# Attention, then a SiLU MLP, on one core: one burst of 64x64 tiles per pair and eight shared PSUM banks

## The chip, the cores and the metric

The kernel runs on one core of one Trainium2 chip. The metric is the device time of one execution in microseconds (us). The kernel before takes 217.31 us, the median of three runs (216.69 to 217.38). TensorE is PE below, VectorE is DVE, ScalarE is ACT, GpSimd is POOL, and SP is the queue that issues most loads.

## The reference

A causal linear attention with decay feeds an MLP with a SiLU. There are 4 batches, 8 heads, 768 positions and a head dimension of 64.

```python
for b in range(nb):                      # blocks of 64 positions
    intra = einsum('bhic,bhjc->bhij', qb, kb) * Dmask
    intra = einsum('bhij,bhjd->bhid', intra, vb)
    inter = einsum('bhid,bhde->bhie', qb * lam_pow, kv_state)
    out[:, :, sl] = intra + inter
    kv_state = lam_block * kv_state + einsum('bhsd,bhse->bhde', kb * rev_pow, vb)
x = out.transpose(0, 2, 1, 3).reshape(3072, 512)
h = x @ w_in                             # 512 -> 2048
return (h * sigmoid(h)) @ w_out          # 2048 -> 512
```

Inputs and output are float32; the kernel's matmuls take bfloat16.

## The kernel before

**Tiling.** Attention works on blocks of 128 positions, two of them (chunks) to a "pair" of 256. There are 12 pairs, three to a batch, and 24 units of 128 tokens for the MLP. For a pair, `prepare` casts k and q into `kq` and scales v into `vd`. It turns k and q into `kqT`: pairs 0 to 3 by PE transposes through a PSUM bank, later pairs by a DMA transpose. `attention` then issues these tiles on PE:

- states (`states`, line 499): 32 matmuls of 64x64 with 64 columns, k against v. The third pair of a batch is final and needs 16.
- scores (`score`, line 561): twice 16 matmuls of 64x64 with 128 columns, k against q. DVE multiplies each half by a triangle into `st` (`mask`, line 566, through the helper at line 300).
- inter (`inter`, line 588): full 128x128 matmuls with 128 columns, q against the carried state in `xe`, which holds two heads on the diagonal of a 128x128 block with zeros beside them.
- outputs (`outputs`, line 598): twice 16 matmuls of 64x64 with 128 columns, v against the masked scores, into the same accumulators as inter. DVE scales them into `xt` (`evac`, line 612).

DVE makes the state chain out of states: `y` is the sum with the carried state (line 527), `xe` the scaled state for inter, `xf` the scaled state for the next chunk.

**The MLP.** `product1` (line 634) forms 2048 hidden columns for a group of 256 or 512 tokens, one PSUM bank at a time, and ACT applies SiLU into `g` (line 650). `product2` (line 670) multiplies a unit by `w_out` in 16 matmuls of 512 columns into one bank. DVE or ACT copies it to `osb`, and ACT's queue stores it.

**PSUM.** Of eight banks, four are a pool `bank`. Two are `st2` for scores, and two are `xd` for inter, outputs and, in other columns, states.

**Order.** `Planner.order` lists the work by an event simulation. Each task has a cost per engine, a key, dependences, and buffers from small pools. An engine that comes free takes the ready task with the lowest key that has its buffers. The resulting order is fixed, and each engine runs its instructions in that order. In the key, attention of pair n stands at about 2n - 5.5, product 1 of a unit u at about u, and product 2 at about u + 4. The planner charges a switch between full matmuls and 64x64 tiles. Loads go through SP's queue in the order of `sequence`, the halves of `w_out` through POOL's queue. `occupy` (line 701) puts matmuls on ones into planned gaps of the first 19 us, but only where the next task's bank has not been written yet.

The keys of outputs and scores are close, so the planner often puts outputs of one unit beside scores of a later one:

```python
de = add((s - 0.7, 0, 2, g) if n else (s - 0.6, 1, g), ... states ...)
sc = add((s + g - 0.7, 0, 3) if i else (s - 0.55, 0), ... score ...)
im = add((s + g + 0.3, 0, 0), ... inter ...)
om = add((s + g + 0.3, 0, 1), ... outputs ...)
```

Of the kernel before, what the change touches and what calls it, by code (L numbers as in the profile page):

```python
# [14 lines left out]
class Task:  # L15
    __slots__ = ("key", "on", "deps", "bufs", "fn", "left", "ready", "end", "users", "nbytes", "kind", "prior", "next", "late")
# [9 lines left out]
class Buf:  # L26

    __slots__ = ("pool", "slot", "left", "tile", "with_")

    def __init__(self, pool, with_=None):  # L30
        self.pool, self.slot, self.left, self.tile, self.with_ = pool, None, 0, None, with_
# [6 lines left out]
class Planner:  # L38
# [6 lines left out]
    SWITCH = 0.095  # L45
    FIRST, LAST, AHEAD = {"SP": 1.15, "ACT": 1.15, "POOL": 3.0}, 1.0, 0.75

    def __init__(self, pools):
        self.pools = {n: list(range(c)) for n, c in pools.items()}
        self.tasks = []  # L50

    def add(self, key, on, fn, deps=(), bufs=(), nbytes=0, kind=None, prior=(), late=0.0):
        key = key if isinstance(key, tuple) else (key,)
        t = Task(key, on, fn, deps, list(bufs) + [b.with_ for b in bufs if b.with_], nbytes, kind, prior, late)
        for b in t.bufs:
            b.left += 1
        self.tasks.append(t)
        return t

    def order(self):  # L60
# [11 lines left out]
        started = set()  # L72
        queues = {e: [] for e in ("SP", "POOL", "ACT")}
        tiled = False
# [50 lines left out]
        while len(out) < len(self.tasks):  # L125
# [6 lines left out]
            while release and release[0][0] <= now:  # L132
                _, _, b = heapq.heappop(release)
                self.pools[b.pool].append(b.slot)
            for e in free:
# [7 lines left out]
                kept, took = [], None  # L143
                while ready[e]:
# [15 lines left out]
                    break  # L160
                for k in kept:
                    heapq.heappush(ready[e], k)
# [4 lines left out]
                for b in t.bufs:  # L167
                    if b.slot is None:
                        b.slot = self.pools[b.pool].pop(0)
                free[e] = now + t.on[e]  # L170
# [24 lines left out]
def kernel(  # L195
# [22 lines left out]
    TIED = 4  # L218
    AWAY, XAWAY, OWN = ((1, 0),), (), (0, 1)
    WKEY, WCAST, WON = -2.0, {"POOL": 1.0, "ACT": 0.6, "DVE": 0.43}, [("POOL", "ACT", "DVE")] * 2 + [("POOL", "DVE"), ("POOL", "ACT")]  # L220
    FIRST_ONES, ONES_UNTIL = 11, 19.0
# [6 lines left out]
    POOLS = dict(bank=4, st2=1, xd=1, raw=11, rawh=6, kq=4, kqT=3, vd=3, st=2, xe=4, y=2, xf=3,  # L228
                 xt2=4, xt4=2, g=40, osb=3, osh=4, one=3, two=2)
    plan = Planner(POOLS)  # L230
    add = plan.add

    def tile_of(b, shape, dt, name):
        if b.tile is None:
            pool = ps if b.pool in ("bank", "st2", "xd") else sb
            b.tile = pool.tile(shape, dt, tag=f"{b.pool}{b.slot}", name=name)
        return b.tile
# [31 lines left out]
    nc.vector.memset(xe_all, 0.0)  # L269
    pose = const.tile([128, 2], F32, name="pose")  # L270
# [56 lines left out]
    def load_pair(key, n, which):  # L327
# [8 lines left out]
        for g, ms in enumerate(parts_of(n)):  # L336
            for i in which:
                bufs[i, g] = Buf("rawh" if n in FINE else "raw")
                ts[i, g] = add((key, g, i), {"SP": 0.55}, lambda e, i=i, g=g, ms=ms: plain(e, i, g, ms), bufs=[bufs[i, g]],
                               nbytes=0.131 * len(ms), kind=WIDE, late=0.3 if n < EARLY else LATE)  # L340
# [3 lines left out]
    def load_w(key, what, j):  # L344
# [7 lines left out]
        for h in range(KI // 2):  # L352
# [5 lines left out]
            t = add((key, 0, h), {"SP": 0.55}, half, bufs=[b], nbytes=0.5243, kind=PLAIN, late=0.1)  # L358
            for ko in (2 * h, 2 * h + 1):
                wload[what, j, ko] = add((WKEY + j, ko), {e: WCAST[e] for e in WON[j]},  # L360
                                         lambda e, b=b, ko=ko: copy(e, w_in_bf[:, ko, cs], b.tile[:, ko % 2]), deps=[t], bufs=[b])
# [47 lines left out]
    def xe_of(b):  # L409
        return xe_all[:, b.slot]  # L410

    def duo_tile(i):
        return tile_of(duo_of[i][0], [128, 2, 512], F32, "xd")
# [3 lines left out]
    def prepare(n):  # L417
# [21 lines left out]
        for g, ms in enumerate(parts):  # L439
            w = len(ms) / 4  # L440
            ck.append([add((s - 1.0, g, i), {"DVE": 0.06 + 0.8 * w, "ACT": 0.17 + 0.9 * w}, lambda e, i=i, g=g: cast(e, i, g),
                           deps=[loads[i, g]], bufs=[bufs[i, g], kq]) for i in range(2)])
            after("k", ck[g])
            cv.append(add((s - 0.8, g), {"POOL": 0.1 + 2.6 * w} if (n, g) in AWAY else {"DVE": 0.12 + 1.15 * w}, lambda e, g=g: scale_v(e, g), deps=[loads[2, g]],
                          bufs=[bufs[2, g], vd]))
            after("v", [cv[g]])

        if n < EARLY:
            def turn(e, bank, i, r, m):
                t = tile_of(bank, [128, 2, NP, U], BF16, "tr")  # L450
                nc.tensor.transpose(t[:, r, m, :], kq_of()[:, i, r, 2 * m:2 * m + 2, :], ident)  # L451

            for g, ms in enumerate(parts):
                w = len(ms) / 4
                turned.append([])
                for i in range(2):
                    bank = Buf("bank")
                    ts = [add((s - 0.7, g, i, r, m), {"PE": 0.056}, lambda e, i=i, r=r, m=m, bank=bank: turn(e, bank, i, r, m),
                              deps=[ck[g][i]], bufs=[bank, kq]) for r in range(2) for m in ms]
                    turned[g].append(add((s - 1.0, 2, g), {"DVE": 0.15 + 1.05 * w, "ACT": 0.17 + 0.85 * w},  # L460
                                         lambda e, i=i, bank=bank, ms=ms: copy(e, t_of()[:, i, :, ms[0]:ms[-1] + 1],
                                                                               bank.tile[:, :, ms[0]:ms[-1] + 1]),
                                         deps=ts, bufs=[bank, kqT]))
# [9 lines left out]

    def attention(n):
# [3 lines left out]
        tied = []  # L478
        if TIED < n + 1 < NU // 2:
            tied = ready_of[n + 1][5][0] + ready_of[n + 1][4]  # L480
# [3 lines left out]
        final = blk == NB - 1  # L484
        own = [Buf("bank"), Buf("bank")] if n in OWN else None
        buf, box = ([], set()) if own else duo(2 * n - 1)
        bufs_d = own or [buf]

        def d_tile(c):
            return tile_of(own[c], [128, 512], F32, "d0")[:, :256] if own else duo_tile(2 * n - 1)[:, c, 256:512]  # L490
# [3 lines left out]
        def states(e, ms):  # L494
            for m in ms:
# [8 lines left out]
        xes = [Buf("xe") for _ in range(1 if final else 2)]  # L504
# [5 lines left out]
        for g, ms in enumerate(parts):  # L510
            w = len(ms) / 4
            de = add((s - 0.7, 0, 2, g) if n else (s - 0.6, 1, g), {"PE": 0.28 * w}, lambda e, ms=ms: states(e, ms), bufs=bufs_d + [kq, vd], kind="tiled",
                     deps=[ck[g][0], cv[g]] + mask_of.get(2 * n - 1, []) + outs.get(2 * n - 1, []))
            sl = slice(ms[0], ms[-1] + 1)
            old = (prev[2][0], last_f) if prev else None
            for c in range(len(xes)):
# [6 lines left out]
                if old:  # L523
                    src = ys[c]

                    def new_y(e, src=src, old=old, d_of=d_of, sl=sl):
# [3 lines left out]
                    sd = [add((s + late - 0.9, 1, g), {"DVE": 0.15 + 0.27 * w}, new_y, deps=[de] + old[1], bufs=[dbuf, src, old[0]])]  # L530
                    so = lambda src=src, sl=sl: src.tile[:, sl]
                b = xes[c]
                made[c] += [add((s + late - 0.9, 2, g), {"POOL": 0.1 + 0.6 * w} if (n, c) in XAWAY else {"DVE": 0.13 + 0.28 * w},
                                lambda e, b=b, so=so, h=h, d=d, sl=sl: mult(e, xe_of(b)[d, sl, 64 * h:64 * h + 64], so()[d],
                                                                             rate[d, sl]),
                                deps=sd, bufs=[src, b]) for h, d in enumerate(halves)]
                if not final:
# [3 lines left out]
                            deps=sd, bufs=[src, f])  # L541
# [4 lines left out]
        if not final:  # L546
            carry[n] = xe[2] + ((xfs[1], fs),)


        half = []  # L550
        for g in range(2):
# [3 lines left out]
            def score(e, g=g, st_ps=st_ps):  # L555
                t = tile_of(st_ps, [128, 2, 2, 2, U], F32, "st_ps")
# [8 lines left out]
            def mask(e, st_ps=st_ps, st=st):  # L565
                mult(e, tile_of(st, [128, 4, 4 * 64], BF16, "st"), st_ps.tile.rearrange("p h m r i -> p (h m) (r i)"),
# [3 lines left out]
                     + (made[0] + made[1] if g and n >= TIED else []), bufs=[st_ps, kqT],  # L570
                     kind="tiled")
            mask_of[i] = [add((s + g - 0.9, 0), {"DVE": 1.25}, mask, deps=[sc], bufs=[st_ps, st])]
# [4 lines left out]
        for g in range(2):  # L577
# [6 lines left out]
            def inter(e, i=i, g=g, used=used, box=box_x):  # L584
                t = duo_tile(i)
                for m in range(2):
# [5 lines left out]
            def outputs(e, i=i, g=g, st=st, box=box_x):  # L592
                t = duo_tile(i)
                for m in range(2):
# [152 lines left out]
```

## Time and profile before

| what | value |
|---|---|
| median of three runs | 217.31 us (216.69 to 217.38) |
| the profiled execution | 217.49 us |
| its span, first to last instruction | 215.6 us |
| mean granted PE clock | 0.984 |
| busy: PE, DVE, ACT, POOL | 205.8, 105.6, 104.3, 19.9 us |
| product 1 on PE (line 634) | 130.0 us in 566 records |
| product 2 on PE (line 670) | 122.0 us in 386 records |
| mask on DVE, 128x1024 | 24 of 1218 ns |
| xt on DVE, 128x512 | 24 of 689 ns |

Matmuls are pipelined, so durations of one group overlap, and their sum is more than the time that PE gives them. Distances between starts say what a matmul costs: in a row, a 512-column matmul comes every 0.216 us and a 256-column one every 0.109 us. A few per cent of the matmul records are missing, and such a hole looks like a wait of about that length.

### The profile page before, as it was taken

Reading aid. Unit: us, or ns where it says so; the run is one execution under the profiler, and the core shown is the slowest. Engines: PE = TensorE matmul, PEld = TensorE weight load, DVE = VectorE, ACT = ScalarE, POOL = GpSimd, SP = SyncE. Lnnn points to the kernel's source line nnn. Section 1 sums busy time; section 2 is a strip of 40 time slices with the busy share of each in tenths; the row PEclk is TensorE's granted clock in tenths of the full one; section 3 lists DMA queues with packets and bytes.
Section 4 is the critical chain, followed back from the end, with each engine's and each line's share of the span. In section 5 each row is a group of like instructions: output and inputs, shape, how many; then the busy total and the mean of one; then the engine's idle time right before and its main releaser. Section 6 shows DMA issues by size and latency. Waiting matters only on the chain.

```text
span 215.6 us, 5080 instructions
## 1 busy us (share of the span) xinstructions
PE 205.8 (95%) x2243; PEld 124.8 (58%) x2267; DVE 105.6 (49%) x161; ACT 104.3 (48%) x151; POOL 19.9 (9%) x34
## 2 busy tenths in 40 slices
PE   7789999999999999999999999999999999999993
PEld 2567788877656566668755545455444444444452
DVE  3888969961728366978958683154111100111000
ACT  4758697955523351547664342442444444444121
POOL 4041326100300000104001030000000000000000
PEclk9967999999999999999999999999999999999999
DMA  4999999999999896999990610110111011110212
GB/s 128 334 381 381 321 348 279 206 216 256 235 349 240 231 351 152 304 269 282 228 287 3 149 52 0 49 52 0 49 52 49 9 40 49 50 53 0 97 49 97
DMA packets 62182, 35.98 MB, mean 167 GB/s; under 512 B 18000, under 2 KB 57168, under 8 KB 62160
## 3 DMA queue, kind: packets, MB, share of 16 engines
q1 hardware_dynamic: 56304, 27.27, 46.9%
q10 hardware_dynamic: 3744, 6.30, 7.8%
q0 software_dynamic: 2112, 2.10, 6.0%
q8 instruction: 17, 0.28, 0.5%
q14 instruction: 5, 0.04, 0.0%
HBM read 27.27 MB, written 6.29 MB: 156 GB/s over the span
## 4 chain that ended last, share of the span: by engine, by line
PE 92%; DVE 4%; issue 2%; ACT 1%; DVEq 0%
PE h_ps L634 39%; PE o_ps L670 38%; PE xd L598 4%; PE idle L705 3%; PE st_ps L561 2%; PE xd L588 2%; PE tr L451 2%; DVE st L300 1%; PE xd L499 1%; DVE xe_all L300 1%; DVE xt L300 1%; ACT g L650 0%; DVE y L527 0%; DVE vd L300 0%; PE d L499 0%
## 5 line engine op out<-in xcount | busy, mean ns | idle before, releaser
L634 PE MATMUL h_ps<-xt,w_in_bf 128*128 128x256 bf16 (+1 forms) x566 | 130.0, 307 | 1.0 <-ACT g L650 0.2
L670 PE MATMUL o_ps<-w_out_bf,g 128*128 128x512 bf16 (+1 forms) x386 | 122.0, 370 | 1.3 <-issue 1.0
L650 ACT ACTIVATE g<-h_ps 128x512 bf16<-128x512 f32 x96 | 70.7, 747 | 83.4 <-PE h_ps L634 81.7
L634 PEld LDWEIGHTS <-w_in_bf 128*128 128x128 bf16 x576 | 55.1, 98 | 29.7 <-issue 0.5
L670 PEld LDWEIGHTS <-g 128*128 128x128 bf16 x400 | 39.1, 98 | 40.6
L300 DVE TENSOR_TENSOR st<-st_ps,tri 128x1024 bf16<-128x1024 f32 x24 | 29.2, 1218 | 14.1 <-PE st_ps L561 14.0
L300 DVE TENSOR_TENSOR xt<-xd,lam_xe 128x512 bf16<-128x512 f32 x24 | 16.5, 689 | 26.5 <-PE xd L598 13.7
L295 DVE COPY osb<-o_ps 128x512 f32<-128x512 f32 x11 | 7.6, 690 | 40.8 <-PE o_ps L670 40.8
L300 POOL TENSOR_TENSOR xf<-y,lam_be 128x256 f32<-128x256 f32 (+1 forms) x12 | 9.9, 822 | 100.2 <-DVE y L527 100.2
L300 DVE TENSOR_TENSOR xe_all<-y,lam_be 64x256 bf16<-64x256 f32 (+1 forms) x34 | 18.4, 540 | 0.6
L293 ACT ACTIVATE osb<-o_ps 128x512 f32<-128x512 f32 (+1 forms) x14 | 7.9, 561 | 15.1 <-PE o_ps L670 14.8
L300 DVE TENSOR_TENSOR vd<-raw,lam_v 128x1024 bf16<-128x1024 f32 (+1 forms) x12 | 14.0, 1163 | 0.5 <-DMA raw<-in_v_dram 0.5
L293 ACT ACTIVATE kq<-raw 128x1024 bf16<-128x1024 f32 (+1 forms) x12 | 12.1, 1010 | 1.9 <-ACT osb L293 0.8
L293 ACT ACTIVATE kqT<-tr 128x1024 bf16<-128x1024 bf16 (+1 forms) x10 | 8.5, 851 | 4.9 <-PE tr L451 4.7
L705 PE MATMUL idle<-ones 128*128 128x128 bf16 (+1 forms) x59 | 9.2, 319 | 1.7 <-DVE ones L247 1.5
L598 PE MATMUL xd<-st,vd 64*64 64x128 bf16 x384 | 10.5, 229 | 0.0
L561 PE MATMUL st_ps<-kqT 64*64 64x128 bf16 x384 | 10.1, 222 | 0.2
L295 DVE CAST kq<-raw 128x1024 bf16<-128x1024 f32 (+1 forms) x14 | 8.8, 629 | 2.9 <-DMA raw<-in_k_dram 2.5
L588 PE MATMUL xd<-kqT,xe_all 128*128 128x128 bf16 x80 | 8.6, 221 | 0.5 <-DVE xe_all L300 0.4
L588 PEld LDWEIGHTS <-xe_all 128*128 128x128 bf16 x80 | 6.5, 99 | 4.1 <-DVE xe_all L300 0.6
L527 DVE TENSOR_TENSOR y<-xd,xf 128x256 f32<-128x256 f32 x13 | 5.4, 418 | 6.2 <-PE xd L499 5.6
L561 PEld LDWEIGHTS <-kqT 64*64 64x64 bf16 x384 | 6.9, 109 | 2.0 <-issue 1.6
(40 smaller groups left out, 63.0 us busy)
## 6 DMA issues: line engine op xcount, KB each, us to landing
out_dram<-osb ACTq DMA_DIRECT2D x23, 256.0 KB, 2.4
raw<-in_k_dram SPq DMA_DIRECT2D x11, 512.0 KB, 6.1
raw<-in_q_dram SPq DMA_DIRECT2D x11, 512.0 KB, 6.8
raw<-in_v_dram SPq DMA_DIRECT2D x11, 512.0 KB, 6.1
raw_w<-in_moe_w_in_dram SPq DMA_DIRECT2D x8, 512.0 KB, 7.4
w_out_bf<-in_moe_w_out_dram POOLq DMA_DIRECT2D x4, 512.0 KB, 13.1
raw<-in_k_dram SPq DMA_DIRECT2D x2, 256.0 KB, 4.8
raw<-in_q_dram SPq DMA_DIRECT2D x2, 256.0 KB, 5.0
```

The lines of the kernel that those rows point to most:

```text
L293: nc.scalar.activation(o, i, AF.Copy)
L295: nc.vector.tensor_copy(o, i)
L300: (nc.vector if e == "DVE" else nc.gpsimd).tensor_tensor(o, a, b, op=AL.mult)
L451: nc.tensor.transpose(t[:, r, m, :], kq_of()[:, i, r, 2 * m:2 * m + 2, :], ident)
L527: nc.vector.tensor_tensor(tile_of(src, [128, NP, 64], F32, "y")[:, sl], d_of(), old[0].tile[:, sl], op=AL.add)
L561: nc.tensor.matmul(t[c, h, m, r, :], lhsT=t_of()[d, 0, r, 2 * g + m, c], rhs=t_of()[d, 1, :, 2 * g + m, c], start=(m == 0 and r == 0), sto ...
L588: nc.tensor.matmul(t[:, c, U * m:U * m + U], lhsT=xe_of(x[0])[:, 2 * g + m, :], rhs=t_of()[:, 1, :, 2 * g + m, halves[c]], start=first_in( ...
L598: nc.tensor.matmul(t[d, c, U * m:U * m + U], lhsT=vd.tile[p, 2 * (2 * g + m) + h, r, :], rhs=st.tile[p, 2 * h + m, U * r:U * r + U], start ...
L634: nc.tensor.matmul(t[:, j, :], lhsT=w_in_bf[:, ko, 128 * m:128 * m + 128], rhs=xt[gi].tile[:, ko, :], start=(ko == 0), stop=(ko == KI - 1))
L650: nc.scalar.activation(t, bank.tile.rearrange("p j (c r a) -> p (j c) r a", c=n // U, r=2), AF.Silu)
L670: nc.tensor.matmul(t, lhsT=g.tile[:, j, 128 * gp:128 * gp + 128], rhs=w_out_bf[:, ko, cs], start=(ko == 0), stop=(ko == KO - 1))
L705: nc.tensor.matmul((t[:, 0] if two else t)[:, 0:w], lhsT=ones[:, 0:128], rhs=ones[:, 0:w], start=True, stop=True)
```

## The change

1. From pair 3 on, one `burst` per pair replaces the separate tasks. It holds inter and outputs of the pair before, then states and scores of its own pair. Each half of the array's rows has a list of its own: rows 0 to 63 states of chunk 0, outputs of chunk 0, scores of the even heads, and rows 64 to 127 outputs of chunk 1, states of chunk 1, scores of the odd heads. The two lists are merged by their running length. The burst is cut into three tasks that follow each other: up to the last output, up to the last score of the first two head pairs, and the rest.
2. Outputs of pair 3 stand in a burst alone (`SOLO`). A last burst has only outputs of pair 11.
3. States of both chunks share one bank, and scores take four. `fence` puts a PE `nop` that waits for the last matmul of chunk 0 ahead of the first state of chunk 1. Masks become four of 128x512 per pair, one per bank.
4. PSUM is one tile of eight banks. When `st2` and `xd` have had their last use, the planner adds their four banks to `bank`. A burst that lacks banks holds back tasks that would take one, except a product 2 when no bank is half filled. Product 1 leaves the last free bank if anything else can go.
5. In pairs 0 and 1 the first state uses are compact: `xs` is 64 columns wide and has no zeros, one DVE instruction makes it instead of two, and inter is 64x64 tiles in two passes with a fence ahead of outputs.
6. v of pair 1 is scaled on DVE and no more on POOL. A few keys are shifted and two casts are given an engine. The SiLU table is loaded by a task of its own. `occupy` uses any vacant bank, and its count per gap is larger. `g` has 36 buffers for 40, and `st` 4 for 2.

```diff
+    SHIFT = {('xe', 0, 0, 1): 4.5, ('load w', 3, 1): -1.5, ('scale', 3, 0): -1, ('xe', 3, 0, 0): 1.5}
+    HOME = {('cast', 3, 0, 1): 'ACT', ('cast w', 1, 3): 'POOL'}
...
+                if not last[b.pool] and b.pool in self.becomes:
+                    to, slots = self.becomes[b.pool]
+                    self.pools[to] += slots
...
                     if any(len(self.pools[p]) < n for p, n in need.items()):
+
+                        held |= t.kind == "burst" and all(len(self.pools[p]) >= n for p, n in need.items() if p != "bank")
+                        kept.append((key, i, t))
+                        continue
+                    if held and "bank" in need and (opened or t.kind != "p2"):
+                        kept.append((key, i, t))
+                        continue
+                    if self.scarce and t.kind == "p1" and "bank" in need and len(self.pools["bank"]) < 2:
+                        spare = spare or (key, i, t)
                         kept.append((key, i, t))
                         continue
...
-    TIED = 4
-    AWAY, XAWAY, OWN = ((1, 0),), (), (0, 1)
-    WKEY, WCAST, WON = -2.0, {"POOL": 1.0, "ACT": 0.6, "DVE": 0.43}, ...
-    FIRST_ONES, ONES_UNTIL = 11, 19.0
+    TIED, SOLO = 3, (3,)
+    AWAY, XAWAY, OWN = (), (), (0, 1)
+    SMALL = (0, 1)
+    WKEY, WCAST, WON = -2.0, {"POOL": 0.75, "ACT": 0.62, "DVE": 0.45}, ...
+    FIRST_ONES, ONES_UNTIL = 10, 19.0
...
+    plan = Planner(POOLS, {"st2": ("bank", [4, 5]), "xd": ("bank", [6, 7])})
+    banks = ps.tile([128, 8, 512], F32, name="banks")
...
+    def fence(done):
+
+        tc.add_manual_dep(nc.tensor.nop(nofuse=True).ins, done[-1].ins.name, mybir.DependencyInfo(
+            mybir.DependencyClass.Sync, mybir.DependencyReason.DATA), reason="rows of one bank")
...
+    def burst(n, alone=False):
...
+            def state(k, r, c):
+                if c and not k and not r:
+                    fence(at_zero)
...
+        if new:
+            queue(0, "d", 64, state, 0)
+        if o:
+            queue(0, "o", 128, output, 0)
+            queue(1, "o", 128, output, 1)
+        elif new:
+            queue(1, "s", 128, score, 1)
+        if new:
+            if not final:
+                queue(1, "d", 64, state, 1)
+            queue(0, "s", 128, score, 0)
+            if o:
+                queue(1, "s", 128, score, 1)
...
+                ts.append(add((2 * n - 8.5 - alone, j), {"PE": order[cut - 1][3] - spent}, go, deps=[t for t in ts[-1:] if t] or deps, bufs=bufs, kind="burst",
+                              tag=("burst", n - alone / 2, j)))
...
-        xes = [Buf("xe") for _ in range(1 if final else 2)]
+        xes = [Buf("xs" if n + c in SMALL else "xe") for c in range(1 if final else 2)]
...
+                if n in SMALL:
+
+                    for y in (1, 0):
+                        for m in range(2):
+                            for c, x in used:
+                                d = halves[y ^ c]
+                                mm = nc.tensor.matmul(t[d, c, U * m:U * m + U], lhsT=xe_of(x[0])[d, 2 * g + m, :],
+                                                      rhs=t_of()[d, 1, :, 2 * g + m, halves[c]],
+                                                      start=first_in(box, c, y ^ c), stop=True, skip_group_check=True)
...
+    table = add((-3.0, 0), {"ACT": 1.28}, lambda e: nc.scalar.preload_act_table_set("silu_and_others"),
+                deps=[lam_x] + ready_of[1][3][0], tag="table")
...
+            elif start < ONES_UNTIL and start - at > 0.15:
+                b = vacant(at, start)
+                if b:
+                    occupy(b, int((start - at) / 0.056 * 0.75), 128)
```

More of the change, by code (lines that the diff above doesn't have):

```diff
@@ L15 @@
 class Task:
-    __slots__ = ("key", "on", "deps", "bufs", "fn", "left", "ready", "end", "users", "nbytes", "kind", "prior", "next", "late")
+    __slots__ = ("key", "on", "deps", "bufs", "fn", "left", "ready", "end", "users", "nbytes", "kind", "prior", "next", "late", "tag")
     def __init__(self, key, on, fn, deps, bufs, nbytes=0, kind=None, prior=(), late=0.0):
@@ L72, in order @@
         started = set()
+        last = {}
+        for t in self.tasks:
+            for b in t.bufs:
+                last.setdefault(b.pool, set()).add(id(b))
+        opened = set()
         queues = {e: [] for e in ("SP", "POOL", "ACT")}
-        tiled = False
+        tiled = self.scarce = False
         clock = [0.0]
@@ L142, in order @@
                     continue
-                kept, took = [], None
+                kept, took, held, spare = [], None, False, None
                 while ready[e]:
@@ L160, in order @@
                     break
+                if took is None and spare and not held:
+                    kept.remove(spare)
+                    took = spare[2]
                 for k in kept:
@@ L593, in outputs @@
                 t = duo_tile(i)
+                follow(i)
                 for m in range(2):
@@ L631, in mm @@
             def mm(e, j, ko, bank=bank, mg=mg):
-                t = tile_of(bank, [128, per, n], F32, "h_ps")
+                t = psum_of(bank).rearrange("p (j n) -> p j n", j=per)
                 m = mg * per + j
@@ L668, in mm @@
                 g, j, _ = gs[gi, ko]
-                t = tile_of(bank, [128, w], F32, "o_ps")
-                nc.tensor.matmul(t, lhsT=g.tile[:, j, 128 * gp:128 * gp + 128], rhs=w_out_bf[:, ko, cs],
+                nc.tensor.matmul(psum_of(bank)[:, :w], lhsT=g.tile[:, j, 128 * gp:128 * gp + 128], rhs=w_out_bf[:, ko, cs],
                                  start=(ko == 0), stop=(ko == KO - 1))
```

261 lines of the change are left out of this document (200 added, 61 removed).

## The prediction

> **What bounds the kernel now.** I read the shares and the chain first, then busy time by stretch, then the order of time on TensorE (PE) in the middle and on VectorE (DVE) early. Page, part 4, the chain that ended last:
>
> ```profile
> PE 92%; DVE 4%; issue 2%; ACT 1%; DVEq 0%
> ```
>
> The stretches (time in the stretch, busy us and instruction count of each engine, granted PE clock, DMA share, GB/s):
>
> ```profile
> 9.00:12.40 3.40, 1.86 (x53) 1.31 (x53) 2.89 (x8) 2.94 (x6) 0.40 (x1) 0.98 1.13 342
> 12.40:19.10 6.70, 6.28 (x87) 5.01 (x87) 5.71 (x11) 3.88 (x6) 1.90 (x1) 0.50 1.07 386
> 19.10:25.30 6.20, 5.73 (x122) 4.32 (x119) 6.05 (x9) 4.89 (x7) 2.09 (x3) 1.00 1.08 360
> 25.30:45.00 19.70, 19.70 (x332) 16.77 (x329) 16.93 (x28) 15.75 (x24) 5.94 (x9) 1.00 1.11 272
> 45.00:155.00 110.00, 108.13 (x1304) 66.03 (x1321) 64.04 (x91) 50.74 (x70) 7.34 (x8) 1.00 0.71 180
> 155.00:212.30 57.30, 56.88 (x293) 27.41 (x295) 5.53 (x8) 20.98 (x31) 0.00 (x0) 1.00 0.12 47
> ```
>
> From 25.3 us on PE is full, so a microsecond counts there only if PE issues less or switches less. From 12.4 to 25.3 DVE is busy 11.76 of 12.9 us, and PE's clock is 0.50 until 19.1.
>
> What attention costs PE in the middle stands in the order of time: start, duration, instruction.
>
> ```profile
> 64.23 0.27 PE L634 MATMUL h_ps<-xt,w_in_bf 128*128 128x256 bf16 x1
> 64.43 0.42 PE L561 MATMUL st_ps<-kqT 64*64 64x128 bf16 x16
> 64.78 0.39 PE L670 MATMUL o_ps<-w_out_bf,g 128*128 128x512 bf16 x1
> ...
> 83.63 0.38 PE L670 MATMUL o_ps<-w_out_bf,g 128*128 128x512 bf16 x1
> 83.84 0.39 PE L588 MATMUL xd<-kqT,xe_all 128*128 128x128 bf16 x4
> 84.16 0.42 PE L598 MATMUL xd<-st,vd 64*64 64x128 bf16 x16
> 84.41 0.42 PE L499 MATMUL xd<-vd,kq 64*64 64x64 bf16 x32
> 84.66 0.40 PE L561 MATMUL st_ps<-kqT 64*64 64x128 bf16 x16
> 84.99 0.61 PE L634 MATMUL h_ps<-xt,w_in_bf 128*128 128x256 bf16 x2
> ```
>
> I call such a run of attention tiles between MLP matmuls a visit. From start to start, 16 outputs or 32 states take 0.25 us, four inter matmuls 0.22. The second visit takes 84.99-83.84 = 1.15 and holds 0.22+3x0.25 = 0.97, so 0.18 goes to entering and leaving the 64x64 form. The lone score visit delays the MLP by 64.78-64.23-0.11 = 0.44 us for one group of 0.25: 0.19. If the groups themselves shrink to the 0.227 that four-deep matmuls would need (16x0.0568/4), the price of a visit is 0.24. I take 0.21.
>
> **Part by part.** The sum is made against the profiled execution: 217.49 us, span 215.6 and 1.9 around it. The median of the three runs shown is 217.31, 0.18 less.
>
> *Bursts, pairs 3 to 11.* Before, these pairs' states, scores, inter and outputs make 23 visits between 37.6 and 155 us. After, there are 11: states and scores of pair 3, outputs of pair 3 alone, states and scores of pair 4, seven full bursts, the last outputs. No matmul goes away. 12 visits x 0.21 = -2.5 us, all on the path since PE is full; bounds -2.2 (0.18) and -2.9 (0.24). In a burst the two row halves run their own lists at once, 64-wide states beside 128-wide outputs. At 76.97 us before, row-0 states and scores of the other row half already overlap in the records, so I keep the array time equal. Masks become four of 128x512 instead of two of 128x1024. The same shape costs 0.69 in the xt groups against 1.22, so DVE gets 4x0.69-2x1.22 = +0.3 us per pair. This is hidden: DVE is busy 64 of 110 us there, and would cost 2.8 us in all were it not.
>
> *The fence in a burst.* States of chunk 1 write the bank of chunk 0's, so a PE nop waits for the last chunk-0 state. It sits in PE's own order, so every output, score and MLP matmul behind it waits too. That state starts about 0.20 us into the tiled part and lasts 0.193 (the states' group), so it ends at 0.39. DVE starts 0.04 to 0.09 after a PE end in this trace, giving 0.43 to 0.48; the outputs ahead of the nop keep row 1 busy until 8x0.0568 = 0.454. No wait of PE on itself is in the trace. Bounds: 0, and one whole states duration, 0.19. A gain is excluded, as nothing is removed. Six bursts have chunk-1 states (final pairs don't): 0 to +1.2 us; I take 0.05 each, +0.3, because the row arithmetic almost covers it.
>
> *Seven banks at once.* A full burst takes two output banks, one for states and four for scores, of eight. While it lacks banks the planner starts no product-1 bank, and a product-2 bank only if none is open. What must drain is a SiLU (0.747 us), an osb copy (0.59 or 0.69), or masks of the forerunner, long done some 12 us later. An open product-2 bank is 16x0.216 = 3.5 us of PE work, longer than any drain. Behind a burst DVE frees banks at 0.69 us each, outputs first; product 1 fills one in 8x0.109 = 0.87. So bounds are 0 and one SiLU plus hop, 0.85, for each of seven full bursts: 6 us. The nearest row is PE waiting for ACT g once, 0.2 us in all. I take +0.4.
>
> *First pairs.* With compact states, pair 0's eight 64x128 products into xe_all become four of full height, and pair 1's first chunk one 128x256 (0.42) instead of two:
>
> ```profile
> 13.69 1.90 POOL L300 TENSOR_TENSOR vd<-raw,lam_v 128x1024 bf16<-128x1024 f32 x1 [1.40 <-DMA raw<-in_v_dram]
> ...
> 14.17 1.56 DVE L300 TENSOR_TENSOR xe_all<-y,lam_be 64x128 bf16<-64x128 f32 x1
> ...
> 21.01 1.58 DVE L300 TENSOR_TENSOR xe_all<-y,lam_be 64x256 bf16<-64x256 f32 x2
> ```
>
> Four halves at 0.286 (the rows from d) saved: -1.1. At 21.0, 1.58 becomes 0.42 to 0.8: -0.9. Pair 1's v scale goes from POOL to DVE, +1.26, but the product that ran beside it on DVE took 1.56 instead of 0.29: -1.27. Together DVE has 2.0 us less before 25.3. Against it, the compact inter needs two passes and a fence before each of four outputs. A matmul there takes 0.229, less 0.11 of the second pass, plus a weight load of 0.11: 0.2 each, partly paid back by the form switch that inter no longer makes. Two lie before PE is full (12 to 16 us), two after 22: +0.4 at most on the path. PE at 19.1 to 25.3 is busy 5.73 of 6.2, so it can't start its full stretch much earlier by DVE alone. I take half of DVE's 2.0: -1.0, bounds -2.0 and +1.0 (nothing saved, all four fences and a later bank paid).
>
> *What moves without a price.* The SiLU table load (1.28) leaves 20.13 for an earlier place on ACT, which idles 2.06 us before 17.02; uncovered it would delay the kqT copy by 1.3. The second half of the last w_in block moves up in SP's queue ahead of pair 2's v: 0.52 MB at 386 GB/s make v 1.4 us later, and DVE reads it only at 28.5. One w_in cast goes to POOL (0.67), ahead of w_out's issues, but product 2 starts at 45.9. Pair 3's q cast goes to ACT, busy 15.75 of 19.70 there. One 512-wide opening dummy less is 0.4 us, ahead of a DMA wait to 5.3. g falls from 40 to 36 buffers, and a pair needs eight. kqT and vd are held until the next burst, three each, so pair n+2 still has a place.
>
> Sum: -2.5+0.3+0.4-1.0 = -2.8, so 217.49-2.8 = **214.7 us**.
>
> **Rivals.**
> *The clock stays full early.* Dummies now go into any vacant bank and fill more of a planned gap. Before, the gap 10.0 to 11.0 has none, and the clock falls at 12.4. If it stays 1.0: three tile groups 0.64 to 0.42, two transposes groups 1.03 to 0.61, inter 0.15, together -1.65 on top: 213.1. Against: DVE is 85% busy there, so much of it would be waited for anyway. The Trainium skill ("TensorE: Matmul & The Clock Gate", Part 1) says half rate comes after an idle window of about 3.4 us. By that rule the clock falls at 12.4 only if 9.0 to 12.4 were idle; PE was busy 1.86 us of it, so the trace doesn't agree to the letter, but by the rule's direction more dummies keep it up, and the sum would be 213.1.
>
> *Banks make the burst late (other side).* The seven banks are not free when the data are, and PE, in its fixed order, stands at the burst's first matmul for a SiLU, or behind the burst for a mask. For: DVE alone empties all seven, 6x0.69+2x0.42 = 5.0 us in a row. Against: the open product-2 bank. At 0.85 us for seven bursts the time is 214.7-0.4+6 = 220.3; at half of it 217.3. It decides from 3.2/7 = 0.46 us per burst. The Trainium skill ("TensorEngine Tiling (Array Packing)", PSUM Bottleneck) warns of this: tiling speeds TensorE, not evacuation, and copies may become the limit; no row of before shows it (PE waits 0.2 us for ACT).
>
> *The early part gets worse.* The new order of first pairs, fences and full-height products delay the first xt. At +1.5 instead of -1.0 the time is 217.2. For: little PE slack from 19.1.
>
> *The bursts don't hold together.* A burst is three tasks; if MLP matmuls go between them, or the row halves don't overlap, seven bursts get two more visits each, 14x0.21 = 2.9: 217.6. Against: a burst that has its banks has an earlier key than the work it interrupts.
>
> **How the numbers follow.** Forecast 0.50 (213.5 to 216.9: the distances of its terms' bounds, the bank waits' left out, added in squares), full clock 0.14, late banks 0.18, worse start 0.12, broken bursts 0.06. Under 0.3% (0.65 us) one can't tell from no change here. Faster, below 216.66: 0.50+0.14+0.06 of the last three cases = 0.70. Within 0.3%: 0.08 from the last two and the lower end of late banks. Slower: 0.22. The range leaves out the upper half of late banks (0.09) and the lowest of the full clock (0.05): 212.4 to 218.6.
>
> **What would show it.** Right: eleven visits from pair 3 on, each full burst about 1.14 (two lists of 0.454+0.454+0.23) +0.45+0.2 = 1.8 us from MLP to MLP; PE full from about 24.3. Wrong: gaps before a burst ended by ACT g or DVE st; a hole of over 0.1 us in the burst at the nop; PE full only after 25.3; a product-1 stretch that waits for DVE behind a burst.

## The result and the profile after

The changed kernel takes 213.43 us (median of four runs, 213.09 to 214.44). The kernel before took 217.0 beside it, so the ratio is 0.984 (95% interval 0.980 to 0.989). The profiled execution took 214.44 us, which is 3.05 less than the profiled execution of before, and its span is 212.7. It was the longest of the four; the other spans are 211.4 to 211.9. The forecast was 214.7, from 212.4 to 218.6.

The chain that ended last and the granted clock, from the page of the changed kernel:

```profile
PEclk9999999999999999999999999999999999999999
...
PE 74%; DMA 15%; SPq 7%; POOL 1%; issue 0%; ACT 0%
```

Each of the 40 slices is 5.3 us; the clock no longer falls in the third and fourth. The chain's DMA share is new: PE waits for a transfer near 51 us, so the chain is followed back from there through DMA and SP's queue instead of through PE.

The stretches of the changed kernel (time in the stretch, busy us and count of PE, PEld (PE's weight loads), DVE, ACT, POOL, clock, DMA share, GB/s):

```profile
9.00:12.40 3.40, 3.35 (x76) 2.83 (x77) 3.38 (x6) 1.65 (x2) 0.00 (x0) 1.00 1.14 342
12.40:19.10 6.70, 5.98 (x141) 4.63 (x138) 5.97 (x13) 5.24 (x7) 3.62 (x5) 1.00 1.07 388
19.10:25.30 6.20, 6.12 (x106) 4.74 (x105) 5.18 (x8) 5.22 (x8) 3.60 (x6) 1.00 1.06 348
25.30:45.00 19.70, 19.22 (x299) 15.52 (x298) 14.40 (x23) 14.70 (x22) 5.14 (x8) 1.00 1.07 268
45.00:155.00 110.00, 109.39 (x1356) 66.70 (x1355) 69.02 (x115) 47.35 (x64) 7.76 (x8) 1.00 0.77 182
```

From 19.1 to 25.3 DVE is busy 5.18 us where it was 6.05, and PE 6.12 where it was 5.73. From 25.3 to 45 PE is no longer quite full.

One full burst in order of time on PE, pair 6's (start, duration, instruction):

```profile
86.31 0.61 PE L554 MATMUL banks<-kqT,xe_all 128*128 128x128 bf16 x8
86.84 0.22 PE L581 MATMUL banks<-vd,kq 64*64 64x64 bf16 x2
86.85 0.24 PE L560 MATMUL banks<-st,vd 64*64 64x128 bf16 x2
...
87.06 0.23 PE L581 MATMUL banks<-vd,kq 64*64 64x64 bf16 x4
87.10 0.41 PE L560 MATMUL banks<-st,vd 64*64 64x128 bf16 x16
87.45 0.22 PE L581 MATMUL banks<-vd,kq 64*64 64x64 bf16 x2
...
87.70 0.63 PE L590 MATMUL banks<-kqT 64*64 64x128 bf16 x32
88.27 0.39 PE L875 MATMUL banks<-w_out_bf,g 128*128 128x512 bf16 x1
```

States of chunk 0 (line 581) and outputs (560) run side by side from 86.84. Then, ahead of the first state of chunk 1 at 87.45, no matmul starts for 0.157 us: that is the fence. The product-2 matmul starts at 88.27, 1.96 us after the first inter.

And the new wait for w_out, PE in the changed kernel:

```profile
49.09 2.13 PE L840 MATMUL banks<-xt,w_in_bf 128*128 128x256 bf16 x18
51.76 0.81 PE L875 MATMUL banks<-w_out_bf,g 128*128 128x512 bf16 x3 [0.54 <-DMA w_out_bf<-in_moe_w_out_dram]
```

PE also waits once for the v of pair 2, by way of DVE, which scales it:

```profile
29.47 1.23 DVE L345 TENSOR_TENSOR vd<-raw,lam_v 128x1024 bf16<-128x1024 f32 x1 [1.59 <-DMA raw<-in_v_dram]
...
30.74 0.44 PE L676 MATMUL banks<-vd,kq 64*64 64x64 bf16 x16 [0.48 <-DVE vd L345]
```

**A ledger.** The starts of product-1 and product-2 matmuls give an account that closes. Their own time is 166.2 us in every kernel here: 560 of 512 columns at 0.216 us and, without the last one, 415 of 256 columns at 0.109 us, the distances measured in a row. The start of the last one is the start of the first, plus 166.2, plus whatever lies between two of them beyond that. I split the latter into visits before 38 us, visits from pair 3 on, and other holes. Up to 26 records are missing from a trace; each hole of 0.216, the length of a 512-column matmul, is taken out as such a record.

| us, profiled executions | first product 1 | early visits | late visits (count) | other holes | last MLP matmul |
|---|---|---|---|---|---|
| before | 19.09 | 7.26 | 18.99 (23) | 0.47 | 211.98 |
| changed | 17.32 | 7.33 | 16.97 (11) | 1.28 | 209.07 |
| difference | -1.77 | +0.07 | -2.02 | +0.81 | -2.91 |

### The profile page after: what moved, and what is told of

Its sections match the earlier page's. It is cut to its first block, busy times and chain, and to the rows that moved or that the text cites. A ratio compares the mean times of both kernels' runs of the same rounds, so it can differ in the third digit from the quotient of the medians.

```text
span 212.7 us, 5266 instructions
## 1 busy us (share of the span) xinstructions
PE 205.6 (97%) x2308; PEld 124.2 (58%) x2308; DVE 106.5 (50%) x179; ACT 99.3 (47%) x142; POOL 22.4 (11%) x38
## 4 chain that ended last, share of the span: by engine, by line
PE 74%; DMA 15%; SPq 7%; POOL 1%; issue 0%; ACT 0%
PE banks L875 38%; PE banks L840 30%; DMA w_out_bf<-in_moe_w_out_dram 8%; SPq L378 5%; DMA raw<-in_k_dram 4%; DMA raw_w<-in_moe_w_in_dram 4%; SPq L403 3%; PE banks L590 2%; PE banks L560 2%; PE banks L581 2%; PE banks L554 1%; POOL w_out_bf L394 1%; POOL w_in_bf L342 0%; ACT osb L338 0%; POOL gate L352 0%
## 5 line engine op out<-in xcount | busy, mean ns | idle before, releaser
L840 PE MATMUL banks<-xt,w_in_bf 128*128 128x256 bf16 (+1 forms) x576 | 116.1, 308 | 0.4 <-POOL w_in_bf L342 0.4
L875 PE MATMUL banks<-w_out_bf,g 128*128 128x512 bf16 (+1 forms) x400 | 112.2, 371 | 0.6 <-DMA w_out_bf<-in_moe_w_out_dram 0.5
L856 ACT ACTIVATE g<-banks 128x512 bf16<-128x512 f32 x96 | 70.2, 745 | 85.0 <-PE banks L840 79.9
L340 DVE COPY osb<-banks 128x512 f32<-128x512 f32 x15 | 10.4, 692 | 56.8 <-PE banks L875 51.3
L345 DVE TENSOR_TENSOR st<-banks,tri 128x512 bf16<-128x512 f32 (+1 forms) x42 | 29.6, 756 | 5.8 <-PE banks L590 4.8
L345 DVE TENSOR_TENSOR xt<-banks,lam_xe 128x512 bf16<-128x512 f32 x24 | 15.7, 686 | 16.3 <-PE banks L560 15.6
L345 DVE TENSOR_TENSOR xe_all<-y,lam_be 64x256 bf16<-64x256 f32 x28 | 14.1, 504 | 0.6
L338 ACT ACTIVATE kq<-raw 128x1024 bf16<-128x1024 f32 x12 | 12.3, 1045 | 1.5 <-DMA raw<-in_k_dram 1.1
L912 PE MATMUL banks<-ones 128*128 128x128 bf16 (+1 forms) x88 | 10.3, 266 | 1.5 <-DVE ones L291 1.5
L560 PE MATMUL banks<-st,vd 64*64 64x128 bf16 x288 | 8.0, 219 | 0.0
```

The costliest lines, as they stand in the source:

```text
L338: nc.scalar.activation(o, i, AF.Copy)
L340: nc.vector.tensor_copy(o, i)
L345: (nc.vector if e == "DVE" else nc.gpsimd).tensor_tensor(o, a, b, op=AL.mult)
L560: nc.tensor.matmul(psum_of(ob[c])[d, U * k:U * k + U], lhsT=o["vd"].tile[halves[c], 2 * k + h, r, :], rhs=o["st"][k // 2].tile[halves[c], ...
L840: nc.tensor.matmul(t[:, j, :], lhsT=w_in_bf[:, ko, 128 * m:128 * m + 128], rhs=xt[gi].tile[:, ko, :], start=(ko == 0), stop=(ko == KI - 1))
L856: nc.scalar.activation(t, psum_of(bank).rearrange("p (jc r a) -> p jc r a", r=2, a=64), AF.Silu)
```

## The experiments

All edits are to the changed kernel unless said otherwise. The ratios are against the kernel before, run beside each group (216.5 us in each).

**bursts_only: undo the first part.**

```diff
-    SHIFT = {('xe', 0, 0, 1): 4.5, ('load w', 3, 1): -1.5, ('scale', 3, 0): -1, ('xe', 3, 0, 0): 1.5}
-    HOME = {('cast', 3, 0, 1): 'ACT', ('cast w', 1, 3): 'POOL'}
+    SHIFT = {}
+    HOME = {}
...
-    AWAY, XAWAY, OWN = (), (), (0, 1)
-    SMALL = (0, 1)
...
-    FIRST_ONES, ONES_UNTIL = 10, 19.0
+    AWAY, XAWAY, OWN = ((1, 0),), (), (0, 1)
+    SMALL = ()
...
+    FIRST_ONES, ONES_UNTIL = 11, 19.0
...
+    table = lam_x
```

The cast costs and the rule of dummies are those of before, too.

> The changed kernel with its first part undone (wide states, v of pair 1 on POOL, shifts, homes, cast costs, table load, dummies as before). Two parts that add up: eleven visits from pair 3 on with a sum near 17.0 us against 19.0, first product-1 matmul near 19.1 as before, granted clock 0.50 for some microseconds again; 2.0 us less than before, 215.0. Rival, the bursts need the early start (or the eight shared banks make new waits): under 1 us less, 216 or more.

Measured 215.3 (0.990, 0.985 to 0.994). The late visits are 11 with 17.08 us, against 16.97, so the bursts' part of the visits stands by itself. In time, the bursts with the old early part gave 1.2 us of the expected 2.0 (215.3 against 216.5). Product 1 did not start at 19.1. It started at 16.65, with the clock at 1.00, and then lost more than that: one early visit of 1.29 where the changed kernel pays 0.44, a hole of 0.76 that ended with a SiLU (ACT), and 1.00 us of waiting for w_out at 46.7. So the start of product 1 is no measure of the early part: what counts is the start together with the holes that follow.

**no_bursts: no burst for any pair.**

```diff
-    TIED, SOLO = 3, (3,)
+    TIED, SOLO = 12, ()
```

> The changed kernel with no bursts at all: every pair has separate tasks, four banks and the two pairs of banks to the end. Two parts that add up: first product-1 matmul stays at 17.3, 20 to 23 visits from pair 3 on with 19 to 20 us, so 2 to 2.5 us above the changed kernel: 215.4 to 216. Rival, the early start alone is given back in the middle (PE waits for w_out or for inputs): 216.7 to 217.3.

Measured 218.12 (1.005, 1.002 to 1.008), worse than either theory and slower than before. Product 1 starts at 17.24, as in the changed kernel. Then there are 28 late visits with 21.55 us, not 20 to 23 with 19 to 20, and two of them wait inside. The changed source also lacks the dependences with which the kernel before made the planner put outputs beside later scores (`hold` and the extra terms of `sc`), so separate tasks scatter more than they did. This run therefore isn't the kernel before with a new first part. Its early part is as good as the changed kernel's (early visits 7.35 us); the visits of the middle, 2.6 us more than before, outweigh it. It doesn't settle the split.

**old_ones and before_ones: the dummies alone.** The first gives the changed kernel the dummies of before, the second the kernel before those of the change.

```diff
-    FIRST_ONES, ONES_UNTIL = 10, 19.0
+    FIRST_ONES, ONES_UNTIL = 11, 19.0
...
+            b = next(b for b in t.bufs if b.pool in PSUM)
             if not at:
-                occupy(vacant(0.5, start), FIRST_ONES, 512)
-            elif start < ONES_UNTIL and start - at > 0.15:
-                b = vacant(at, start)
-                if b:
-                    occupy(b, int((start - at) / 0.056 * 0.75), 128)
+                occupy(b, FIRST_ONES, 512)
+            elif start < ONES_UNTIL and start - at > 0.2 and id(b) not in seen:
+                occupy(b, int((start - at) / 0.08 * 0.75), 128)
```

> The changed kernel with the dummies of before (11 at the start, only into the next task's unwritten bank, two thirds as many per gap). Clock theory: the granted clock falls to 0.50 somewhere in 9 to 19 us, the first product-1 matmul comes 0.6 to 1.7 us later than 17.3, and the time is 214.1 to 215.2. Rival, DVE's and ACT's smaller early load made the start: product 1 starts at 17.3 to 17.6 whatever the clock, time 213.2 to 213.8.

Measured 213.64 (0.982, 0.978 to 0.987), with the clock at 0.999 or 1.000 in all four runs and product 1 at 17.54. The numbers are the rival's, but the clock theory's case, a fall of the clock, did not come up. In these four executions the changed kernel kept the clock without its dummies. PE is somewhat fuller ahead of the place where the clock fell before, 2.34 us where it was 1.86, as the stretch of old_ones shows:

```profile
9.00:12.40 3.40, 2.34 (x64) 2.07 (x62) 2.55 (x4) 1.65 (x2) 0.00 (x0) 1.00 1.09 329
```

> The kernel before with the changed rule of dummies alone (any vacant bank, more per gap, 10 at the start). Clock theory: granted clock 1.00 from 12.4 to 19.1, first product-1 matmul at 18.0 to 18.5 instead of 19.1, time 216.0 to 216.5. Rival, DVE or ACT sets the start: the clock stays up and product 1 still starts at 18.8 to 19.1, time 216.8 to 217.3.

Measured 216.47 (0.998, 0.995 to 1.001): no difference in the median. Its profiled execution looks like the clock theory: product 1 starts at 18.00, the span is 214.6 instead of 215.6, and the clock stays up where it was 0.50:

```profile
12.40:19.10 6.70, 5.23 (x135) 4.30 (x133) 6.63 (x12) 4.93 (x7) 1.90 (x1) 1.00 1.03 363
```

The explanation is in the runs of before. Of the 51 beside the three groups of experiments, 13 have a mean clock of 0.984 and spans of 215.6 to 216.1 us; the other 38 have 0.990 or more and spans of 214.0 to 215.3. The profiled execution of before, with 0.984 and 215.6, was of the kind of the 13. So the fall of the clock costs about 1.2 us, in a quarter of its executions, and the median hardly knows of it. (Two of the four executions of before that ran beside the result, 217.31 and 217.38, have times of that kind; against 216.5 the changed kernel's ratio would be 0.986.) None of the ten runs of before_ones has the fall. With a quarter as the rate that could still be chance (0.75 to the tenth is 0.06). The same holds for the dummies of before in the changed kernel: the four runs of old_ones and the four of bursts_only have no fall, and chance alone would give that with 0.10. That the changed kernel doesn't need its dummies is likely, not shown.

The Trainium skill ("TensorE: Matmul & The Clock Gate", Part 1) describes the activity window as free-running, not started by the kernel. The 13 of 51 agree with that: in the same program the clock falls in some executions and not in others. Five of the other 38 have 0.990 to 0.992, so perhaps a shorter fall, with spans of 214.7 to 215.1.

**late_fence: states of chunk 1 last in their list.**

```diff
-            if not final:
-                queue(1, "d", 64, state, 1)
             queue(0, "s", 128, score, 0)
             if o:
                 queue(1, "s", 128, score, 1)
+            if not final:
+                queue(1, "d", 64, state, 1)
...
-            de = bursts[1]
+            de = bursts[1] if final else bursts[2]
```

> The changed kernel with states of chunk 1 last in the second row list (after scores), so that the fence comes about 0.45 us after the last state of chunk 0 has ended. If the hole of 0.157 us in the burst is the wait for that state: the four full bursts with a fence go from 1.97 and 1.74 us to about 1.85 and 1.62, visits from pair 3 on sum to 16.4 to 16.6 instead of 16.97, time 0.4 to 0.5 less (213.0). Rival, the nop costs this wherever it stands: 1.97 and 1.74 again, 213.4.

Measured 212.63 (0.980, 0.975 to 0.984). The four full bursts with a fence go from 1.97 and 1.74 to 1.82 and 1.60 us, with missing records taken out, and the late visits sum to 16.46. That is 0.5 us; the median fell by 0.8, and the rest is within the spread, since the intervals of the two kernels overlap. The same burst on PE in late_fence:

```profile
86.02 0.41 PE L560 MATMUL banks<-st,vd 64*64 64x128 bf16 x16
86.24 0.22 PE L590 MATMUL banks<-kqT 64*64 64x128 bf16 x2
...
86.46 0.41 PE L590 MATMUL banks<-kqT 64*64 64x128 bf16 x16
86.69 0.19 PE L581 MATMUL banks<-vd,kq 64*64 64x64 bf16 x2
86.71 0.22 PE L590 MATMUL banks<-kqT 64*64 64x128 bf16 x2
```

The nop stands ahead of 86.69, about half a microsecond after chunk 0's last state has ended, and matmuls follow without the hole. So the hole was the wait for the last state of chunk 0, not the nop. With it gone, a burst with both chunks costs what one of a final pair costs, which has no states of chunk 1 and no fence (1.81).

**solo_all: every pair's outputs in a burst of their own.**

```diff
-    TIED, SOLO = 3, (3,)
+    TIED, SOLO = 3, tuple(range(3, 11))
```

> The changed kernel with every pair's outputs in a burst of their own: seven more visits, and never more than five banks at once. Visit price from the two traces, (18.99-16.01)/12 = 0.25 us: 18 visits, 18.7 us instead of 16.97, time 1.7 more (215.1). Rival, seven banks at once cost waits that this takes away: 1 us more or less than that, 214.4 or below.

Measured 214.78 (0.991, 0.988 to 0.995), 1.35 above the changed kernel. There are 17 late visits, not 18, since the last two output bursts fell together at 138 us. They take 18.39 us, so six more visits cost 1.42, or 0.24 each. Taking the seven-bank demand away gave nothing back, so the full bursts were not waiting for banks.

**wout_early: w_out's loads one load earlier.**

```diff
-    sequence = "u0 u1 i0 i1 u2k i2 u2q u2v i3 u3v u3k g3k o0 u3q o1 o2 o3".split()
+    sequence = "u0 u1 i0 i1 u2k i2 u2q u2v i3 u3v u3k g3v o0 u3q o1 o2 o3".split()
```

> The changed kernel with w_out's loads released by the landing of pair 3's v, one load ahead of its k. If PE's one wait in the middle (0.54 to 0.71 us near 51 us, ended by w_out's DMA) is all that it costs: no such hole, 0.5 to 0.7 less, 212.8. Rival, the transfer only takes its share from pair 3's q and pair 4's loads, and PE waits for those instead: 213.4 or more, with a new hole at 38 to 63 us.

Measured 213.17 (0.983, 0.978 to 0.988), 0.26 below the changed kernel, with intervals that overlap. No hole ended by w_out is in its profile. But late_fence and solo_all, which issue w_out as the changed kernel does, don't show it either. They have a hole of 0.73 or 0.59 at 17.5 us instead, ended by a w_in cast on POOL. So the wait is there in some executions and not in others with the same loads, and that the earlier load is worth anything is not shown.

**no_compact: wide states in pairs 0 and 1, all else as changed.**

```diff
-    SMALL = (0, 1)
+    SMALL = ()
```

> The changed kernel with wide states in pairs 0 and 1 too (two DVE products into a 128-wide block, full inter matmuls, no fence there). My sum: DVE has 2.0 us more before 25 us, half of it on the path, 0.4 of fences come back: product 1 starts later or has holes before 30 us, 0.6 to 1.0 more, 214.0 to 214.4. Rival, DVE has slack there now and the fences were the dearer: 213.0 to 213.5.

Measured 219.34 (1.012, 1.009 to 1.015), 5.9 above the changed kernel, far outside both expectations. PE has early visits of 2.61, 3.41 and 1.46 us. The DVE order of no_compact shows why:

```profile
25.68 1.26 DVE L345 TENSOR_TENSOR xe_all<-y,lam_be 64x256 bf16<-64x256 f32 x2
26.97 0.69 DVE L340 CAST kq<-raw 128x1024 bf16<-128x1024 f32 x1
27.69 0.58 DVE L345 TENSOR_TENSOR xe_all<-y,lam_be 64x128 bf16<-64x128 f32 x1
```

The last 64x128 product belongs to pair 0, whose products `SHIFT` holds back by 4.5 in the key. Pair 1's inter needs it and starts at 28.3, where the changed kernel's starts at 20.2. So in large part the run measures a shift that doesn't fit the wide form, and I took the shift out in the next two.

**no_shift_xe and no_compact2: the same comparison without that shift.**

```diff
-    SHIFT = {('xe', 0, 0, 1): 4.5, ('load w', 3, 1): -1.5, ...}
+    SHIFT = {('load w', 3, 1): -1.5, ...}
```

with `SMALL = ()` as well in the second.

> The changed kernel without the one key shift that holds pair 0's second xe product back. no_compact showed pair 1's inter waiting until 28.3 us for that product. If the shift only suits the compact form: here PE has few new holes, start 16.6 to 17.4, time 213 to 214. Rival, the order that this shift makes is itself what the early gain is: 215 or more.

> The same without the shift, and with wide states in pairs 0 and 1: compact alone is the difference to no_shift_xe. My sum: 0.6 to 1.0 above no_shift_xe (2.0 us of DVE before 25 us, half on the path, 0.4 of fences back). Rival, the fences were as dear as the products: within 0.4 of it. In both, product 1 starts between 16.6 and 17.6.

Measured 215.16 (0.993, 0.991 to 0.995) and 216.52 (1.000, 0.998 to 1.003). Product 1 starts at 16.54 and 16.50, a little before the expected range. With compact states the one key is worth 1.7 us: without it PE has a gap of 1.10 at 16.9 (two dummies, and 0.83 of waiting for a w_in cast on POOL) and a hole at 24.7, where in no_shift_xe

```profile
25.99 1.25 PE L840 MATMUL banks<-xt,w_in_bf 128*128 128x256 bf16 x10 [1.04 <-DVE xt L345]
```

PE stands for an xt that DVE reached at 25.25, behind casts and products that the planner now put first. So the rival held. Compact states are worth 1.36 us in the medians of this pair, more than the 0.6 to 1.0 I gave them; the profiled spans differ by only 0.6, and the order changes with the edit. With wide states the same key costs 2.8 us (219.34 against 216.52). So the key is tuned to the compact form: with it the two give 3.1 us (216.52 to 213.43), of which the form alone gives 1.4.

**pool_scale: v of pair 1 scaled on POOL.**

```diff
-    AWAY, XAWAY, OWN = (), (), (0, 1)
+    AWAY, XAWAY, OWN = ((1, 0),), (), (0, 1)
```

> The changed kernel with v of pair 1 scaled on POOL again. My sum: 1.26 us less on DVE, but the DVE product beside it takes up to 1.27 longer, so nothing: within 0.5 of the changed kernel, 213.0 to 213.9, and a stretched DVE product (0.3 to over 1 us) next to POOL's 1.9 us. Rival, POOL's 1.9 us delays vd of pair 1 and with it states and outputs: 0.6 or more above, 214.0 and up.

Measured 213.82 (0.986, 0.983 to 0.990), 0.39 above, inside what the first theory gave. POOL and DVE in pool_scale:

```profile
14.87 1.90 POOL L345 TENSOR_TENSOR vd<-raw,lam_v 128x1024 bf16<-128x1024 f32 x1 [11.71 <-DMA raw<-in_v_dram]
...
15.05 1.87 DVE L345 TENSOR_TENSOR xf<-y,lam_be 128x128 f32<-128x128 f32 x1
```

A DVE product that takes 0.29 us alone (in the kernel before) takes 1.87 here and ends 0.15 behind POOL's. Product 1 starts at 18.31, 1.0 later than in the changed kernel, but the other holes of its profile sum to 0.20 instead of 1.28, with no wait for w_out. The medians differ by 0.39, and their intervals overlap. The Trainium skill ("SBUF — State Buffer", Who interferes with whom) says that a VectorE instruction with two SBUF inputs contends with a GpSimd instruction that reads SBUF. Both inputs of this product, y and lam_be, are in SBUF, and the trace agrees.

**late_fence_wout: the two moves together.**

> Both moves: states of chunk 1 last in their list, and w_out's loads one load earlier. late_fence alone gave 212.63. If w_out's wait is a matter of the load's place: 212.2 to 212.4 and no hole near 51 us in any profile. Rival, that wait varies from execution to execution and is not always there: 212.6 again.

Measured 212.44 (0.980, 0.976 to 0.983), the fastest here. Its stretches:

```profile
25.30:45.00 19.70, 19.70 (x317) 15.87 (x317) 14.90 (x23) 14.34 (x21) 5.13 (x8) 1.00 1.13 270
45.00:155.00 110.00, 110.00 (x1360) 67.08 (x1350) 66.73 (x111) 49.53 (x69) 7.48 (x8) 1.00 0.79 184
```

PE is never idle between 25.3 and 155 us, the late visits are 16.36 us with no record missing, and other holes sum to 0.43. It is about 1.0 us below the changed kernel (0.980 against 0.984 of before; the intervals overlap a little). Against late_fence alone (212.63) the difference is within the spread, so the two theories about w_out's wait stay undecided.

## Why the prediction was right

The forecast was 2.8 us less and the profiled executions differ by 3.05. The sum came out through terms that erred both ways, and the closeness is in part luck. The profiled execution of before has the fall of the clock, 1.2 us that three in four don't have, and the profiled one of the changed kernel has two waits for loads, 0.48 and 0.71 us on PE, that the profiles of late_fence, solo_all and old_ones, with the same loads, lack. Without either, before takes 216.4 us (median of the 38) and the other three of the changed kernel 213.1 to 213.7.

- **Visits, -2.5 (-2.2 to -2.9).** The mechanism and the counts were right: 23 and 11. The price was too low. The late visits without six fences of 0.16 are 16.01 us, so 12 visits fewer saved 18.99-16.01 = 2.98, or 0.25 each; solo_all gives 0.24. This is a hair beyond the upper bound, which assumed that the matmuls of a group run four deep at 0.0568, and in the bursts they do. The lower bound took the wait between groups for the groups' own time. That the price is of the visit and not of what runs side by side in a burst is shown by solo_all, which has the same matmuls in more visits.
- **Fences, +0.3 (0 to 1.2).** Mis-sized. Six fences cost 0.16 each (1.97 against 1.81, and 1.07 against 0.91 for states and scores alone in solo_all), so +0.96. I had chunk 0's last state start at 0.20 us and be over at 0.39. In the trace it starts 0.25 into the tiled part and is over at 0.44. From there to the next matmul's start it is another 0.17, where I had put the 0.04 to 0.09 of DVE behind a PE end: the weight load of the first state of chunk 1 starts at 87.42, and its matmul follows at 87.45. The cover of 0.454 ends before that. My own sign of being wrong here, a hole of over 0.1 us at the nop, did come. late_fence removed the hole by moving the nop.
- **Seven banks at once, +0.4 (0 to 6).** Nothing. No wait for a SiLU or a mask stands ahead of or behind a burst in the changed kernel's trace, and solo_all, which never needs seven, gains nothing. The rival of late banks fell. What the Trainium skill ("TensorEngine Tiling (Array Packing)", PSUM Bottleneck) warns of, copies out of PSUM as the limit, no run here shows.
- **First pairs, -1.0 (-2.0 to +1.0).** In the ledger the start and the early visits give -1.7 against the profiled before. About 1.1 of that is the clock, by before_ones. The rest, some 0.6, is the order, the compact states and the move of v together. It is 0.6 with the wait for pair 2's v in it; in the profile of wout_early, which has the same early order without that wait, start and early visits are 23.95 us against 25.34 in before_ones, 1.4 less. The parts cannot be added up: the one key is worth 1.7 us with compact states and costs 2.8 with wide ones. My sum of DVE durations gave the right sign and size, and the products shrank as summed (pair 0's from eight with 3.5 us to four with 1.1). But DVE is busy 18.96 us up to 25.3, where it was 19.08: other work moved into the time. How much of the gain comes from the shorter products and how much from the order is not shown.
- **What moves without a price.** Two of these had one in the profiled execution. I named product 2's start at 45.9 as w_out's cover (it was 45.7); product 2 now starts at 43.4, and PE waited for w_out, 0.54 us by the profile and 0.71 from start to start. The load that moved ahead of pair 2's v was to cost nothing since DVE read that v only at 28.5: in the profiled execution DVE waited for it until 29.5, and PE 0.48 us behind it. With them, PE is busy 19.22 of 19.70 us from 25.3 to 45, so a sign of being wrong that the prediction names, PE full only after 25.3, came in this execution. In late_fence_wout PE is full there (19.70).

The rival of the full clock came true in the profile but not in the median, because before is mostly at full clock too. Broken bursts didn't happen: each burst is one visit.

## What to carry to other kernels

Where PE is full, count the changes between full matmuls and small tiles, not the matmuls: here each visit cost about 0.25 us on average, and merging twelve away gave 3.0 us, of which the fences took back 1.0. A wait inside such a run belongs as far behind its producer as the list allows; moving one list entry saved about 0.15 us in each of four places. And before explaining a difference between two profiled executions, ask whether the event is in every execution: the clock's fall was in one of four. And an order tuned to one form can harm another: the same key saves 1.7 us with compact states and costs 2.8 with wide ones.

## What the runs showed of the hardware that I had not expected

- The same program has a mean PE clock of 0.984 in 13 of 51 executions (in a profiled one of this kind, 0.50 for 6.7 us) and 0.990 or more in the other 38, 33 of them 0.997 or more. The 13 take about 1.2 us longer. The changed kernel with fewer dummies (PE busy 2.34 of 3.40 us ahead of the place) kept the clock in four of four.
- With a PE nop that waits for a PE matmul, no matmul starts for 0.157 us where the awaited one ends just then; where it had ended about 0.5 us earlier (late_fence), the trace shows no hole.
- States of 64 columns on one row half and outputs of 128 columns on the other ran side by side without a loss that shows: a final burst's tiled part takes 76.96-75.70 = 1.26 us from its first state to the next MLP matmul, against the prediction's 1.14 for the longer list alone. About 0.1 of the 1.26 is leaving the 64x64 form, by the kernel before, where the next MLP matmul starts 0.15 us after the last score and scores start 0.05 apart.
